# A list scheduler's priorities shifted by fixed, hashed offsets in 33 stretches of its operation list

## The chip, the cores and the metric

The kernel runs on one core of a Trainium2 chip. That core has five engines that this kernel uses: TensorE (PE in the profile, with PEld for its weight loads), VectorE (DVE), ScalarE (ACT), GpSimd (POOL), and SyncE (SP), which issues the transfers. Each engine works through its own queue of instructions in order, and engines wait for one another through semaphores. The metric is the device time of one execution in microseconds; the median over several runs is what is compared.

## The reference

Two attention layers are computed over 2048 tokens of width 1024, with 32 heads of 32, and their outputs are concatenated.

```python
# A: causal softmax attention in 4 segments of 512, plus a memory M, z carried from segment to segment
q, k, v = x @ wq, x @ wk, x @ wv                 # per head
for s in range(4):
    p = softmax(qs @ ks.T * scale + mask);  a_dot = p @ vs
    a_mem = (phi(qs) @ M) / (phi(qs) @ z + 1e-6)          # phi(t) = t + 1 if t > 0 else exp(t)
    outs.append(g * a_mem + (1 - g) * a_dot)              # g = sigmoid(beta), one a head
    M, z = M + phi(ks).T @ vs, z + phi(ks).sum()
a = concat(outs) @ wo
# B: linear attention with a learned map and two softmaxes over 32 features
pq, pk = q @ w_phi, k @ w_phi
phi_q = concat(softmax(pq), softmax(-pq));  phi_k = concat(softmax(pk), softmax(-pk))
kv, z = phi_k.T @ v, phi_k.sum()
b = ((phi_q @ kv) / (phi_q @ z + 1e-6)) @ wo
out = concat([a, b], axis=-1)
```

## The kernel before, in words

Every large product is made of float16 halves: an operand is scaled, its float16 rounding is the high half and the remainder the low half, and three products (high by high, high by low, low by high) are added in PSUM. Three of the products (q and k of B, v of B, the output of A) are also done by a Strassen scheme of seven products on half-size blocks (`strassen`, and `mult` at the end of the kernel), whose sums are made on DVE, ACT and POOL.

The work has five stages, in this order of time:

- **The opening.** Loads of x and of the first weights, their scaling into halves (`load_seg`, `load_wg`, `load_wv`, all through `halved` and `halves`), while PE runs products of the identity to keep busy (L1079).
- **Stage A.** 32 units, each one segment and one group of four heads. `produce(u)` projects q, k and v of a unit (L378) and `attend(u)` does its attention: row maxima (L796 on PE, L802 on DVE), scores (L894), exponentials (L898, L900 on ACT), masks (L907 on POOL), and the product with v (L930). In the background the weights of B are folded with the feature map (`fold`, L1035).
- **The change from A to B.** The V projection of two pairs of token blocks is taken ahead (`xpair` with the Strassen form made on POOL and ACT, L477 and L484, after a scaling at L546), while the last units of A attend.
- **The K pass of B.** Eight pairs of blocks: Strassen for k and v (L574), two softmaxes (`expo`, L1140 to L1154), and the sums over tokens (L1294). At its end the sums are turned into the operands of the next stage (L1317 and around).
- **The Q pass of B, and the output of A.** For 16 token blocks the same for q, then the transposed features times the sums (L1475), and the output projection of B (`project`, L378). Last come 8 pairs of blocks of A's output by Strassen (`mult`, L1539).

None of this order is written out engine by engine. The code calls `Graph.op` once for every operation (16,483 in all), in program order, with an engine, an expected duration, a function that emits the instructions, the buffers read and written, and a priority `prio`: a small number is to go first. In stage A the priority is 2u for `produce(u)` and 2u + 1 for `attend(u)`; in B it is 100 plus two for each pair of K, then one for each block. `Graph.op` stores `(prio, place in the list)` in `o.prio`. At the end `Graph.run` plays the whole list through in planned time: at each step it takes the engine that can start first, and of the operations that are ready there it emits the one with the smallest `o.prio`:

```python
            some = [x for x in lists[e] if start(x) <= t + 1e-9]
            if e == "PE":
                some = [x for x in some if safe(x) <= t + 1e-9] or some
            o = min(some, key=lambda x: x.prio)
```

So the priority decides only between operations that are ready at the same planned moment; data dependences, buffers and PSUM banks hold whatever the priority is. Every emission fixes a place in an engine's queue. Where the planner foresees PE idle for more than `GAP = 0.5` us, `fill` (L336) emits some products of the identity into a free PSUM bank, at most one per 0.22 us of four fifths of the gap; they compute nothing that is used. They are instructions that depend on the order.

SP's transfers stand in the same list: one queue, in planned order.

Of the kernel before, what the change touches and what calls it, by code (L numbers as in the profile page):

```python
# [41 lines left out]
WPLAN = ((None, 0, 0), (None, 2, 1), (None, 3, 5), ((1, 0, "subtract"), 0, 3), ((3, 1, "subtract"), 1, 4),  # L42
         ((3, 0, "subtract"), 3, 2), ((2, 3, "subtract"), 2, 6))
EUP = 2.0 ** 15


def view(t, off, ap):
# [13 lines left out]


class Op:
    __slots__ = ("eng", "dur", "fn", "prio", "lat", "deps", "wait", "ready", "short", "port", "banks", "place", "known", "safe", "kb")


class Graph:
# [36 lines left out]
    def op(self, eng, dur, fn, r=(), w=(), prio=0, lat=0.0, short=False, port=False, need=(), kb=256):  # L104
        o = Op()
        o.short, o.port = short, port or eng == "POOL"
        o.eng, o.dur, o.fn, o.prio, o.lat, o.kb = eng, dur, fn, (prio, len(self.ops)), lat, kb
        o.banks = []
        ends, starts = set(), set()
        for b in need:  # L110
            if b.prev[0] is not None:
                ends.update(b.prev[0].ops)
        for write, accs in ((0, r), (1, w)):
            for acc in accs:
                b, key = acc if isinstance(acc, tuple) else (acc, None)
                old, last, opened = b.prev
                if old is not None:
                    ends.update(old.ops)
                if not b.ops and last is not None:
                    starts.add(last.ops[0])  # L120
                if opened is not None:
                    starts.add(opened)
                for k in (list(b.writer) if key is None else [key, None]):
                    if k in b.writer:
                        ends.add(b.writer[k])
                if write:
                    for k in (list(b.readers) if key is None else [key, None]):
                        ends.update(b.readers.pop(k, ()))
                    if key is None:
                        b.writer.clear()  # L130
                    b.writer[key] = o
                else:
                    b.readers.setdefault(key, []).append(o)
                b.ops.append(o)
                if b.kind is not None and b not in o.banks:
                    o.banks.append(b)
                    b.left += 1
        ends.discard(o)
        o.deps = [(d, 0) for d in ends] + [(d, 1) for d in starts - ends if d is not o]
        self.ops.append(o)  # L140
        return o

# [115 lines left out]
SP, PE, ACT, DVE, POOL = "SP", "PE", "ACT", "DVE", "POOL"  # L258
# [3 lines left out]
def tile_kernel(ctx: ExitStack, tc: tile.TileContext, ax, aw, awv, awo, beta, bx, bwqk, bwv, bphi, bwo, out):  # L262
# [69 lines left out]
    for t in vfb:  # L332
# [7 lines left out]
    gate1 = const.tile([128, H], F32, name="gate1")  # L340
    gates = G.fixed(gate)
    op(SP, 0.6, lambda: nc.sync.dma_start(gate, bass.AP(tensor=beta.tensor, offset=beta.offset, ap=[[0, 128], [1, H]])),
       w=[gates], prio=0.2, lat=2.0, kb=16)
    op(ACT, 0.2, lambda: nc.scalar.activation(gate, gate, AF.Exp, bias=0.0, scale=-1.0), w=[gates], prio=0.2)
    op(DVE, 0.2, lambda: nc.vector.tensor_scalar(gate, gate, 1.0, None, op0=OP.add), w=[gates], prio=0.2)
    op(DVE, 0.3, lambda: nc.vector.reciprocal(gate, gate), w=[gates], prio=0.2)
    op(DVE, 0.2, lambda: nc.vector.tensor_scalar(gate1, gate, -1.0, 1.0, op0=OP.mult, op1=OP.add), w=[gates], prio=0.2)
# [779 lines left out]
    def expo(ps, prio, sk, up=None):  # L1127
        port = ps not in psums

        def x3():  # L1130
            return ps().rearrange("p (h d) -> p h d", d=32)

        def rep(v):
            return v[:, :, None].to_broadcast([128, 16, 32])

        mx = G.buf("b", [128, 2, 16], F32, "mx", 2)
        e = G.buf("b", [128, 16, 2, 32], F32, "e", 5)
        r = G.buf("b", [128, 16, 2], F32, "r", 5)
        for i, o in ((0, OP.max), (1, OP.min)):
            op(DVE, 0.6, lambda i=i, o=o: nc.vector.tensor_reduce(mx()[:, i, :], x3(), axis=AX.X, op=o),  # L1140
               r=[ps], w=[(mx, i)], prio=prio)
        op(DVE, 0.6, lambda: nc.vector.tensor_tensor(e()[:, :, 0, :], x3(), rep(mx()[:, 0, :]), op=OP.subtract),  # L1142
           r=[ps, (mx, 0)], w=[(e, 0)], prio=prio, port=port)
        op(DVE, 0.6, lambda: nc.vector.tensor_tensor(e()[:, :, 1, :], rep(mx()[:, 1, :]), x3(), op=OP.subtract),  # L1144
           r=[ps, (mx, 1)], w=[(e, 1)], prio=prio, port=port)
        for i in range(4):
            op(ACT, 0.41, lambda i=i: nc.scalar.activation(  # L1147
                e()[:, 4 * i:4 * i + 4], e()[:, 4 * i:4 * i + 4], AF.Exp, bias=0.0, scale=sk()[:, i:i + 1]),
               r=[e, sk], w=[(e, ("x", i))], prio=prio)
        op(DVE, 1.13, lambda: nc.vector.tensor_reduce(r(), e(), axis=AX.X, op=OP.add), r=[e], w=[r], prio=prio)  # L1150
        op(DVE, 0.27, lambda: nc.vector.reciprocal(r(), r()), r=[r], w=[r], prio=prio)
        if up is not None:
            op(POOL, 0.2, lambda: nc.gpsimd.tensor_scalar(r(), r(), up, None, op0=OP.mult), r=[r], w=[r], prio=prio)
        return e, r  # L1154

    def bc32(r):
        return r()[:, :, :, None].to_broadcast([128, 16, 2, 32])
# [84 lines left out]
    for p in range(NT // 2):  # L1242
# [9 lines left out]
        def kout(i, hb, ps, es=es, sk=sk, P=P):  # L1252
            e, r = expo(ps, P, sk, EUP)
            op(POOL, 1.95, lambda: nc.gpsimd.tensor_tensor(e(), e(), bc32(r), op=OP.mult), r=[e, r], w=[e], prio=P)
            es[i, hb] = e
# [58 lines left out]
    for q in range(4):  # L1314
        ps = bank("misc", [128, 512])
        for i in range(4):
# [3 lines left out]
        op(ACT, 0.5, lambda q=q, ps=ps: nc.scalar.activation(  # L1320
            zb()[:, 4 * q:4 * q + 4, :].rearrange("p a b -> p (a b)"), ps(), AF.Copy, scale=1.0 / EUP), r=[ps], w=[(zb, q)], prio=P)
    op(DVE, 0.1, lambda: nc.vector.tensor_scalar(osc2[:, 1, 0:1], big[:, 1:2], 2.0, None, op0=OP.mult),
# [299 lines left out]
```

## Time and profile before

| | |
|---|---|
| median of 3 runs | 1735.99 us (1734.22 to 1736.42) |
| span of the profiled execution | 1738.3 us, 2.3 us above that median |
| PE busy | 1696.5 us, 98% of the span |
| DVE busy | 1394.7 us, 80% |
| ACT busy | 1140.9 us, 66% |
| POOL busy | 961.8 us, 55% |
| mean granted TensorE clock | 0.995 of full |
| transfers | 275.71 MB, mean 159 GB/s |

The page of the profile gives, in this order, the busy time by engine, the span in 40 slices, the transfer queues, the chain of work that ended last, and the costliest groups of instructions. The same trace can be asked for the busy time of each engine in any stretch, for instructions in order of time, and for who waited for whom. A matmul is shown with the time until its result is out (380 ns for 512 columns), and the next may start before that; so a PE that is shown busy may still start fewer matmuls than it could. An idle PE is shown only where a gap is longer than that tail.

### The profile page before, as it was taken

What the parts mean: (1) busy time and instruction counts of PE and PEld (TensorE: products, weight loads), DVE (VectorE), ACT (ScalarE), POOL (GpSimd) and SP (SyncE); (2) the same over time, 40 slices, a digit from 0 to 9 for tenths busy, and PEclk for the clock granted to TensorE, in tenths of its full rate; (3) what the DMA queues carried; (4) which work ended last, traced back from release to release, by engine and by line L of the source; (5) the groups of instructions that cost most, each with busy time, mean ns of one, the idle gap of its engine ahead of it and who ended that gap; (6) DMA issues with size and microseconds to landing.
All of it is one profiled execution on the core that took longest, in us unless ns stands there. A gap on an engine that the chain in (4) does not pass through costs nothing. (4 is left out here: it accounts for less than half of the span.)

```text
span 1738.3 us, 38775 instructions
## 1 busy us (share of the span) xinstructions
PE 1696.5 (98%) x14604; PEld 1027.0 (59%) x14604; DVE 1394.7 (80%) x3197; ACT 1140.9 (66%) x2083; POOL 961.8 (55%) x1301
## 2 busy tenths in 40 slices
PE   8999999999999999999999999999999999999998
PEld 6767767667776767766754444444544444454443
DVE  6989889789878878788885999996998777696441
ACT  6987887888778776878765767654664554454331
POOL 6446354445757775867755545453588898541000
PEclk9999999999999999999999999999999999999999
DMA  6546545457544643565466443346555774576311
GB/s 203 192 133 173 154 143 177 146 163 233 153 148 136 150 130 113 161 209 149 128 202 241 141 164 128 128 164 233 217 146 146 172 193 134 128 206 171 110 65 61
DMA packets 240844, 275.71 MB, mean 159 GB/s; under 512 B 137488, under 2 KB 190480, under 8 KB 231952
## 3 DMA queue, kind: packets, MB, share of 16 engines
q1 hardware_dynamic: 240656, 273.22, 51.8%
q8 instruction: 115, 1.88, 0.5%
q14 instruction: 73, 0.60, 0.1%
HBM read 145.44 MB, written 85.00 MB: 133 GB/s over the span
## 5 line engine op out<-in xcount | busy, mean ns | idle before, releaser
L378 PE MATMUL proj<-S,S 128*128 128x512 f16 (+1 forms) x3072 | 499.8, 300 | 2.8 <-ACT S L405 0.7
L378 PEld LDWEIGHTS <-S 128*128 128x128 f16 x4608 | 330.6, 98 | 150.5 <-issue 5.5
L574 PE MATMUL proj<-S,S 128*128 128x512 f16 x1488 | 345.4, 380 | 9.2 <-ACT cs L580 4.9
L574 PEld LDWEIGHTS <-S 128*128 128x128 f16 x1968 | 187.0, 98 | 224.9 <-issue 10.4
L907 POOL TENSOR_SCALAR_AFFINE_SELECT ph<-ph 128x256 f16<-128x256 f16 (+1 forms) x448 | 193.5, 453 | 167.3 <-DVE ph L901 148.1
L901 DVE SCALAR_TENSOR_TENSOR ph<-s,ph 128x512 f16<-128x512 f32 x320 | 210.3, 684 | 66.1 <-ACT ph L900 64.0
L802 DVE CUSTOM_DVE_ANT_0 s<-s,causal 128x256 f32<-128x256 f32 (+3 forms) x512 | 242.5, 509 | 16.5 <-PE s L796 13.2
L898 ACT ACTIVATE s<-s,bd 128x512 f32<-128x512 f32 x320 | 211.8, 705 | 25.1 <-PE s L894 23.1
L900 ACT ACTIVATE ph<-s 128x512 f16<-128x512 f32 x320 | 189.3, 651 | 0.9
L378 PE MATMUL misc<-S,ot 128*128 128x512 f16 x768 | 170.7, 379 | 0.0
L1147 ACT ACTIVATE e<-e,sk 128x256 f32<-128x256 f32 x256 | 114.5, 498 | 84.8 <-DVE e L1144 81.1
L378 PEld LDWEIGHTS <-ot 128*128 128x128 f16 x768 | 73.7, 98 | 87.6
L796 PE MATMUL s<-S 96*128 96x512 f16 (+3 forms) x512 | 113.3, 299 | 3.1 <-DVE mt L802 1.5
L894 PE MATMUL s<-S 104*128 104x512 f16 (+3 forms) x512 | 113.8, 299 | 1.1 <-DVE mt L802 0.9
L1444 POOL TENSOR_TENSOR e<-e,zb 128x512 f32<-128x512 f32 x64 | 84.9, 1340 | 44.9 <-DVE r L1150 38.8
L378 PE MATMUL proj<-wv,S 128*128 128x128 f16 x1536 | 107.9, 220 | 1.0 <-DVE mt L802 0.7
L930 PEld LDWEIGHTS <-ph 128*128 128x128 f16 x2560 | 87.4, 96 | 16.6 <-issue 1.8
L930 PE MATMUL pv<-vl,ph 128*128 128x66 f16 (+1 forms) x2560 | 92.6, 184 | 1.9 <-POOL ph L907 0.8
L1150 DVE TENSOR_REDUCE r<-e 128x32 f32<-128x1024 f32 x64 | 76.7, 1203 | 15.9 <-ACT e L1147 15.8
L574 PE MATMUL s<-S,S 128*128 128x512 f16 x324 | 77.4, 379 | 0.0
L1287 POOL TENSOR_TENSOR pt<-e,pt 128x512 f16<-128x512 f32 x32 | 38.6, 1209 | 65.9 <-ACT pt L1284 63.2
L802 DVE DVE_READ_ACCUMULATOR2_ANT mt<- 128x1 f32 x512 | 71.8, 140 | 0.0
(330 smaller groups left out, 3313.1 us busy)
## 6 DMA issues: line engine op xcount, KB each, us to landing
S<-h SPq DMA_DIRECT2D x192, 128.0 KB
S<-wf_d SPq DMA_DIRECT2D x21, 1024.0 KB
st<-bwqk SPq DMA_DIRECT2D x64, 256.0 KB
wf_d<-fo SPq DMA_DIRECT2D x48, 256.0 KB
out<-os SPq DMA_DIRECT2D x39, 256.0 KB
wf_d<-oT SPq DMA_DIRECT2D x36, 256.0 KB
S<-xf_d SPq DMA_DIRECT2D x9, 1024.0 KB
S<-aw SPq DMA_DIRECT2D x16, 512.0 KB
```

The lines of the kernel that those rows point to most:

```text
L378: op(PE, dur, lambda c=c, a=a, b=b, lv=lv, rv=rv: nc.tensor.matmul(pv(), lv(), rv(), start=(c == 0 and a + b == 0), stop=(c == n - 1 and a ...
L574: op(PE, 0.215, lambda n=n, a=a, b=b, lv=lv, rv=rv: nc.tensor.matmul(ps(), lv(), rv(), start=(start and n == 0 and a + b == 0), stop=(n == ...
L796: nc.tensor.matmul(ps()[:, o:o + 128 * i + 128], st()[0:96, 0, h, 128 * i:128 * i + 128], st()[0:96, 1, h, 0:128 * i + 128], start=True, s ...
L802: dve(0.12 + 0.00113 * n, lambda h=h, i=i, o=o, n=n: nc.vector.tensor_tensor_reduce(ps()[:, o:o + n], ps()[:, o:o + n], causal[:, 512 - n: ...
L894: nc.tensor.matmul(ps()[:, o:o + n], st()[0:104, 1, h, 128 * j:128 * j + 128], st()[0:104, 0, h, 128 * j:512], start=True, stop=True)
L898: act(0.59, lambda: nc.scalar.activation(ps(), ps(), AF.Exp, bias=0.0, scale=bd()[:, 4, i2, 0:1]), r=[(bd, i2)], w=[ps])
L900: act(0.5, lambda: nc.scalar.activation(ph()[:, 0], ps(), AF.Copy, scale=2.0 ** 14), r=[ps], w=[(ph, 0)])
L901: dve(0.6, lambda: nc.vector.scalar_tensor_tensor(ph()[:, 1], ps(), 2.0 ** 14, ph()[:, 0], op0=OP.mult, op1=OP.subtract), r=[ps, (ph, 0)], ...
L907: nc.gpsimd.affine_select(pd, pd, pattern=[[0, n], [1, 128]], compare_op=OP.is_ge, fill=0.0, base=0, channel_multiplier=-1)
L930: nc.tensor.matmul(ps()[:, i, n0:n1], ph()[:, a, o:o + 128], vl()[:, j, h, n0:n1], start=(i == 0 and a == 0), stop=(j == min(i, 2)), skip_ ...
L1147: op(ACT, 0.41, lambda i=i: nc.scalar.activation(e()[:, 4 * i:4 * i + 4], e()[:, 4 * i:4 * i + 4], AF.Exp, bias=0.0, scale=sk()[:, i:i + 1 ...
L1444: op(POOL, 1.35, lambda a=a, h0=h0, e=e: nc.gpsimd.tensor_tensor(e()[:, 8 * a:8 * a + 8], e()[:, 8 * a:8 * a + 8], zv()[:, h0:h0 + 8], op= ...
```

## The change

Every operation gets an offset on its priority if it lies in one of 33 chosen stretches of 60 operations in the list. The offset is a hash of the operation's place and of the stretch's number in a table, scaled to plus or minus 0.3, 0.7, 1.5 or 3.0 (chosen by the last two bits of that number). Matmuls that follow one another with the same priority, code and bank share one place, and so one offset, so that a run of matmuls into one bank stays together. The chosen stretches are 0, 3, 4 and 5 (the opening), ten between 162 and 178 (the last units of A and the first products of B), eleven between 207 and 227 (the end of the K pass and the first blocks of Q), and eight between 251 and 260 (the last blocks of Q and the first of A's output). Durations, dependences, buffers, and the functions that emit instructions are as they were.

```diff
+STRETCH, REACH = 60, (0.3, 0.7, 1.5, 3.0)
+NUDGE = {0: 102925, 3: 583361, 4: 334074, 5: 356900, 162: 548157, 166: 12065, 167: 23722, 168: 590453, 170: 363531, 172: 857500,
...
+         254: 713827, 257: 574795, 258: 625840, 259: 632051, 260: 875719}
 class Op:
-    __slots__ = (..., "known", "safe", "kb")
+    __slots__ = (..., "known", "safe", "kb", "at", "base")
+def nudge(at):
+    seed = NUDGE.get(at // STRETCH, 0)
+    if not seed:
+        return 0.0
+    x = (at * 2654435761 & 0xFFFFFFFF) ^ (seed * 2246822519 + 374761393 & 0xFFFFFFFF)
...
+    return REACH[seed & 3] * (2 * (x / 4294967296.0) - 1)
 def op(self, eng, dur, fn, ...):
...
+        o.base, o.at = prio, len(self.ops)
+        last = self.ops[-1] if self.ops else o
+        if o.eng == "PE" and (last.eng, last.base, last.fn.__code__, last.banks) == (o.eng, prio, fn.__code__, o.banks):
+            o.at = last.at
+        o.prio = (prio + nudge(o.at), len(self.ops))
         self.ops.append(o)
```

More of the change, by code (lines that the diff above doesn't have):

```diff
@@ L63 @@
 class Op:
-    __slots__ = ("eng", "dur", "fn", "prio", "lat", "deps", "wait", "ready", "short", "port", "banks", "place", "known", "safe", "kb")
+    __slots__ = ("eng", "dur", "fn", "prio", "lat", "deps", "wait", "ready", "short", "port", "banks", "place", "known", "safe", "kb", "at", "base")
+def nudge(at):
[3 more added lines that the diff above has]
+    x = (at * 2654435761 & 0xFFFFFFFF) ^ (seed * 2246822519 + 374761393 & 0xFFFFFFFF)
+    x ^= x >> 15
+    x = x * 2246822519 & 0xFFFFFFFF
+    x ^= x >> 13
+    x = x * 3266489917 & 0xFFFFFFFF
+    x ^= x >> 16
+    return REACH[seed & 3] * (2 * (x / 4294967296.0) - 1)
 class Graph:
```

2 rows, old and new, of the table NUDGE are left out of this document.

## The prediction

> **What bounds the kernel now.** I read the busy times first, then the time in stages, then the planner's idle-time products in the same stages, then the instructions in order of time around the waits, and last the order of the two built programs. The page says PE:
>
> ```profile
> span 1738.3 us, 38775 instructions
> PE 1696.5 (98%) x14604; PEld 1027.0 (59%) x14604; DVE 1394.7 (80%) x3197; ACT 1140.9 (66%) x2083; POOL 961.8 (55%) x1301
> L336 PE MATMUL fill<-ident 128*128 128x128 f32 x148 | 23.6, 305 | 0.0
> ```
>
> PE is idle for 1738.3 − 1696.5 = 41.8 us, and 23.6 us of its busy time are fills (L336), which compute nothing. The next fence has the busy time in eight stretches, which I cut at the opening and the changes of stage, and the same for fills alone. The columns are length, then busy us and count for PE, PEld, DVE, ACT and POOL, the granted clock, the transfers' share and GB/s; the fills' rows have PE and PEld only.
>
> ```profile
> 0.00:40.00 40.00, 35.15 (x251) 26.90 (x252) 26.39 (x69) 28.39 (x40) 25.16 (x36) 0.96 0.58 191
> 40.00:870.00 830.00, 818.98 (x8947) 583.55 (x8945) 713.26 (x2070) 656.09 (x1191) 501.38 (x798) 1.00 0.54 158
> 870.00:930.00 60.00, 54.57 (x425) 33.15 (x424) 43.73 (x103) 40.17 (x71) 40.70 (x56) 0.94 0.62 199
> 930.00:1220.00 290.00, 281.87 (x1824) 138.04 (x1823) 251.77 (x412) 175.21 (x353) 133.66 (x125) 1.00 0.48 173
> 1220.00:1305.00 85.00, 80.35 (x628) 45.15 (x627) 80.86 (x137) 53.72 (x114) 58.35 (x62) 1.00 0.56 170
> 1305.00:1520.00 215.00, 214.31 (x1391) 101.15 (x1389) 164.07 (x241) 106.17 (x188) 175.03 (x197) 1.00 0.61 155
> 1520.00:1580.00 60.00, 58.16 (x403) 29.40 (x401) 47.76 (x67) 27.67 (x47) 27.51 (x31) 1.00 0.66 177
> 1580.00:1738.27 158.27, 153.07 (x749) 69.61 (x747) 66.82 (x99) 53.46 (x82) 0.00 (x0) 1.00 0.29 103
> ...
> 0.00:40.00 40.00, 4.41 (x22) 3.74 (x22) 0.96 0.58 191
> 870.00:930.00 60.00, 7.18 (x40) 6.44 (x40) 0.94 0.62 199
> 930.00:1220.00 290.00, 1.05 (x8) 1.05 (x8) 1.00 0.48 173
> 1220.00:1305.00 85.00, 7.24 (x50) 6.20 (x50) 1.00 0.56 170
> 1520.00:1580.00 60.00, 3.71 (x28) 3.52 (x28) 1.00 0.66 177
> ```
>
> The reader should see that PE's loss, idle time plus fills, is dense in short places. From A to B it is 5.43 + 7.18 = 12.6 us in 60; from K to Q 4.65 + 7.24 = 11.9 in 85; from Q to A's output 1.84 + 3.71 = 5.6 in 60; in the opening 4.85 + 4.41 = 9.3 in 40. Stage A and the K pass lose 11.0 and 8.1 us of idle time spread over 1120 us, and 1305 to 1520 only 0.7. DVE is busy 80.86 of 85 us from K to Q, so there it, and not PE, sets the pace.
>
> What ends the waits in these places (start, duration, engine, line; idle time before it and its releaser in brackets):
>
> ```profile
> 896.57 2.03 PE L336 MATMUL fill<-ident 128*128 128x128 f32 x16
> 899.59 1.12 PE L574 MATMUL proj<-S,S 128*128 128x512 f16 x4 [1.00 <-ACT S L484]
> 902.03 0.59 PE L822 MATMUL misc<-identr,mh 128*8 128x128 f16 x4 [1.32 <-DVE mh L817]
> 902.55 2.08 PE L336 MATMUL fill<-ident 128*128 128x128 f32 x8
> 897.89 1.13 ACT L546 ACTIVATE wv<-wv,pst 128x1024 f32<-128x1024 f32 x1
> 898.92 1.65 ACT L484 ACTIVATE S<-wv 128x512 f16<-128x512 f32 x3
> ...
> 1266.03 0.38 SPq L561 DMA_DIRECT2D S<-xf_d  x1
> 1273.49 2.76 PE L574 MATMUL proj<-S,S 128*128 128x512 f16 x12 [1.15 <-DMA S<-xf_d]
> 1283.85 2.05 PE L336 MATMUL fill<-ident 128*128 128x128 f32 x16
> 1550.12 1.83 PE L336 MATMUL fill<-ident 128*128 128x128 f32 x14
> 1568.97 2.75 PE L1539 MATMUL proj<-S,S 128*128 128x512 f16 x12 [1.46 <-ACT S L1556]
> ```
>
> From A to B, PE sits through 8 fills (16 passes, since a float32 product takes two) and 1.00 us more until ACT has scaled the second x block (L546) and rounded its first forms (L484). From K to Q it waits for a transfer that SP issues at 1266.03. At the end of Q it fills between the blocks' sums and output products.
>
> **What the change moves.** All 16,483 planned operations stay, so no work is removed but fills. Their order was compared in the built programs: on PE, 8140 of 9740 operations have another place (by at most 228); on DVE 2452 of 2675, on ACT 1745 of 1988, on POOL 1037 of 1286, on SP 600 of 793 (by at most 19). The first PE move is at its 67th operation, and everything after that follows, chosen stretch or not. The fills, counted as instructions by place:
>
> ```
>                     opening  stage A  A to B  K pass  K to Q  Q to out   all
> fills before           11       0       20      4      25       14       74
> fills after            11       2        4      4      15        0       36
> ```
>
> A fill stands only where the planner found no ready PE work for over 0.5 us, so the new order has ready work in about half of those places. That is no time; I price it by the rows.
>
> *Opening: 0.* The fills stay 11. On PE, the first v product moves behind the second half of the q product. On POOL, five small operations (three of L351, one L764, one L727) move ahead of the second weight group's halves.
>
> ```profile
> 34.63 1.16 POOL L402 TENSOR_TENSOR S<-S,S 128x512 f16<-128x512 f32 x1 [1.38 <-ACT S L401]
> 38.84 2.27 POOL L402 TENSOR_TENSOR S<-S,S 128x512 f16<-128x512 f32 x2
> 41.22 1.27 POOL L764 TENSOR_TENSOR pk<-pk,z 128x512 f32<-128x512 f32 x1
> 43.16 2.55 POOL L351 TENSOR_TENSOR bdm<-hd,gate 128x128 f32<-128x128 f32 x7
> 45.68 0.57 POOL L727 TENSOR_SCALAR sc<-gate,bv 128x4 f32<-128x4 f32 x2
> 40.42 0.81 PE L378 MATMUL proj<-S,S 128*128 128x512 f16 x3
> 47.94 4.48 PE L378 MATMUL proj<-S,S 128*128 128x512 f16 x20
> ```
>
> They cost 3 × 0.36 + 1.27 + 0.29 = 2.6 us. The first half group was ready at 34.63 + 1.16 = 35.8 and is wanted at 40.42; the second was ready at 38.84 + 2.27 = 41.1 and is wanted by 47.94. Both slacks, 4.6 and 6.8, cover 2.6. If L764, now ahead, also waits for its exponential, the cover of the first is gone and PE waits up to 2 us. I take 0, with ends −1 (the q half done earlier) and +2.
>
> *A to B: −5.7.* L546 stands 32 to 34 places earlier on ACT, its scale matmul (L521) 75 places earlier on PE, and the first products of V (L574) 88 to 106 places earlier; the key update of the unit before (L869) stands 70 later, ready work for the gap. On POOL the last fold's forms (L477, L485) move up to 28 places back and the second V pair's up to 28 ahead, for the same PE products; SP's transfers here move by at most 8 places. So the wait at 896 to 900 loses its cause. 16 fills fewer × 7.18 / 20 = 5.7 us. At best half of the 5.43 us idle there (2.7) and the lost clock go too (60 × 0.06 = 3.6): −12. At worst the waits stay without fills: 0.
>
> *K to Q: −2.9.* The sums (L1294, L1317) are mixed with Strassen products; 10 fills fewer × 7.24 / 25 = 2.9. The transfer at 1266.03 keeps its place in SP's queue: here only two stores move by more than 2 places. So the 1.15 us stay, and the 8 fills before the first output products (L378) are still there. Ends: 0, and −5 with half of the idle time.
>
> *Q to A's output: −3.7.* All 14 fills go; the output products (L378) now stand between the sums (L1475) and the first products of A's output. 3.71 us; ends 0 and −4.6 (with half of 1.84).
>
> *Stage A and the K pass: +0.6, and a new draw.* Two new fills × 23.6 / 74 = 0.6. Besides, 11.0 + 8.1 = 19.1 us of small waits fall anew, since these orders change too. I see no direction in it; between a quarter less and a quarter more, ±5. The longest of them also slowed the clock:
>
> ```profile
> 336.40 1.08 PE L864 MATMUL misc<-ident,pk 128*128 128x128 f32 x4 [2.57 <-DVE mt L802]
> 340.00:342.00 2.00, 2.00 (x8) 0.76 (x6) 1.38 (x4) 0.00 (x0) 0.00 (x0) 0.50 0.81 151
> 304.22:347.68 43.46, 40.47 (x430) 27.56 (x428) 34.72 (x93) 36.09 (x67) 20.19 (x40) 0.92 0.46 146
> ```
>
> After 2.57 us of waiting PE ran at half clock; the slice lost 0.08 × 43.46 = 3.5 us of clock.
>
> *Sum.* 0 − 5.7 − 2.9 − 3.7 + 0.6 = −11.7, the fills' own time. PE does not get all of it: where a fill goes, a short wait under 0.5 us can stand, which the planner does not count. In the trace idle time outside the opening and the tail (41.8 − 4.85 − 5.2 = 31.8) is larger than the fills outside the opening (23.6 − 4.41 = 19.2), so more waits are unforeseen than foreseen. I take off a third: −8. The end does not move: after 1580 PE is full (its 5.2 us idle is the last store) and in both programs the same products remain. 1738.3 − 8 = 1730.3 for the profiled execution; it stood 2.3 above the median, so 1728.0.
>
> **Rivals.**
> *The waits go with their fills, and more.* All better ends: −1 − 12 − 5 − 4.6 − 5 = −27.6, around 1708; half of that beyond the forecast is 1718. For it: the bracketed waits lie beside the fills that go. Against: DVE at 80.86 of 85 us.
>
> *Nothing that counts.* The gain in three places, −8, is given back by the new draw, +5, and the opening, +2: 1735. For it: 84% of PE's operations move, so waits that the old order happened to hide can open anywhere in 1120 us, and from K to Q DVE is full whatever PE's order is.
>
> *Slower: the waits stay, the fills go, and the clock falls.* Place: 870 to 930 and 1220 to 1305. Without fills PE idles where it was kept busy, and each half-clock stretch costs what the slice above lost, 3.5 us. With two or three more of them, +7 to +10: 1743 to 1746. It decides from the point at which PE's idle time in these two places exceeds its present 10.1 us by the 8.6 us that the fills gave up. Against it: the L546 move takes the cause of the longest wait away. [...]
>
> **How the numbers follow.** Forecast (1721 to 1732): 0.55. More (below 1721): 0.17. Nothing that counts (1732 to 1740): 0.13, of which 0.02 and 0.01 lie just outside the bound that follows. Slower (above 1740): 0.15. What a measurement of this kernel can tell from no change is about 0.2%, 3.5 us: 1732.5 to 1739.5. Faster 0.74, same 0.10, slower 0.16. The range 1715 to 1740 leaves out the outer part of the second case (0.05) and the last one (0.15).
>
> **What would show it.** Fills of about 72 passes and 11 to 12 us. From A to B no wait for L484 above 1 us and a clock near 1.00. K to Q still with a wait for xf_d and DVE full. No fills and no wait for L1556 at the end of Q. Wrong would be: PE's idle time in the three places above 15 us, a new half-clock stretch, or a wait over 2 us for POOL's weights near 40 us.

## The result and the profile after

The changed kernel takes 1726.93 us (median of 4 runs, 1723.14 to 1728.99) against 1735.58 us for the kernel before (median of 4, 1734.22 to 1736.42). The ratio is 0.9947, with a 95% interval of 0.9933 to 0.9962: 6.6 to 11.6 us less. The forecast was 1728.0.

The head of the changed kernel's page (lines of this kernel stand 24 further down: L360 is the fill that was L336):

```profile
span 1721.4 us, 38599 instructions
PE 1682.5 (98%) x14528; PEld 1014.9 (59%) x14528; DVE 1397.0 (81%) x3197; ACT 1145.5 (67%) x2083; POOL 966.6 (56%) x1301
```

The eight stretches of the prediction, cut where PE had done the same matmul work, with the columns as there:

```profile
0.00:40.50 40.50, 33.64 (x259) 25.91 (x260) 26.67 (x73) 29.60 (x42) 25.52 (x39) 1.00 0.64 202
40.50:867.40 826.90, 817.62 (x8877) 580.06 (x8876) 713.42 (x2069) 659.31 (x1191) 500.41 (x794) 1.00 0.53 159
867.40:916.70 49.30, 47.19 (x422) 29.17 (x421) 40.40 (x98) 39.35 (x70) 35.73 (x51) 1.00 0.62 205
916.70:1210.80 294.10, 284.47 (x1849) 139.85 (x1848) 253.22 (x412) 173.55 (x348) 138.74 (x133) 0.99 0.49 174
1210.80:1295.30 84.50, 77.54 (x619) 42.89 (x617) 83.51 (x145) 54.24 (x119) 56.28 (x61) 1.00 0.57 184
1295.30:1509.70 214.40, 214.40 (x1393) 101.22 (x1392) 172.84 (x248) 108.72 (x192) 181.19 (x200) 1.00 0.63 167
1509.70:1564.30 54.60, 54.60 (x374) 26.18 (x374) 38.56 (x56) 27.48 (x44) 28.70 (x30) 1.00 0.53 148
1564.30:1721.39 157.09, 153.10 (x750) 69.65 (x747) 68.34 (x101) 53.25 (x81) 0.00 (x0) 1.00 0.28 101
```

And the fills alone, in the stretches that have any (PE and PEld only):

```profile
0.00:40.50 40.50, 3.32 (x22) 2.84 (x22) 1.00 0.64 202
40.50:867.40 826.90, 0.69 (x4) 0.52 (x4) 1.00 0.53 159
867.40:916.70 49.30, 1.05 (x8) 0.97 (x8) 1.00 0.62 205
916.70:1210.80 294.10, 1.22 (x8) 1.21 (x8) 0.99 0.49 174
1210.80:1295.30 84.50, 4.25 (x30) 3.73 (x30) 1.00 0.57 184
```

The stretch from A to B is 49.3 us long instead of 60, and the one at the end of Q 54.6 instead of 60, with PE busy in all of it. The K pass is longer, 294.1 instead of 290. From K to Q DVE is busy 83.51 of 84.5 us, against 80.86 of 85.

The two profiled executions differ by 16.9 us, twice what the runs differ by. The changed one is the fastest of its four runs; the one of before, at 1738.3, was slower than every one of that kernel's four runs. So single stretches of two profiles are read here only together with the runs.

For that I use one more quantity. A matmul's usual step is the distance between starts that the kernel before shows when nothing is in the way (216 ns for 512 columns). **Loss** is the start time of a matmul minus the steps of all matmuls before it; fills count as no work. So it holds waits, fills and time at a lower clock together. All kernels below do 1641.1 us of steps, so losses can be compared at the same work. The table has the loss that each stretch adds; "open" is the first 250 us of steps (the opening and the first units of A), then the marks are 800, 900, 1150, 1300 and 1450 us of steps. Each row is one execution; the last column is the ratio of times to the kernel before, from several runs.

```
                 fills  open    A   A-B     K   K-Q    Q   end    all    ratio (95%)
before              74  19.9  20.6  16.2  12.9  14.7  2.3   4.8   91.3
after               36  23.7  14.0   6.0  16.9  13.3  1.4   0.4   75.7   0.9947 (0.9933-0.9962)
opening alone       91  25.7  16.0  16.7   8.1  15.3  2.5   4.5   88.7   1.0004 (0.9995-1.0013)
A to B alone        60  19.4  16.1  12.8  14.5  14.5  2.3   4.7   84.2   0.9981 (0.9973-0.9990)
K to Q alone        56  19.4  16.9  14.0  11.1  13.3  1.4   2.8   78.9   0.9969 (0.9957-0.9981)
end of Q alone      60  20.4  18.4  14.7  12.3  14.6  1.5   0.4   82.3   0.9966 (0.9953-0.9979)
K to Q + end        46  20.2  17.8  16.0  11.9  13.3  1.5   0.4   81.0   0.9949 (0.9935-0.9962)
all but opening     31  20.4  18.4  13.2  12.5  13.4  1.7   0.4   79.9   0.9938 (0.9925-0.9950)
```

In the changed kernel's row the loss falls most in stage A, from A to B and at the end, and it rises before 250 us of steps and in the K pass. Its 75.7 against 91.3 is more than the runs differ by, since these are the two profiled executions above.

### The profile page after: what moved, and what is told of

Its sections match the earlier page's. It is cut to its first block, busy times and chain, and to the rows that moved or that the text cites. A ratio compares the mean times of both kernels' runs of the same rounds, so it can differ in the third digit from the quotient of the medians.

```text
span 1721.4 us, 38599 instructions
## 1 busy us (share of the span) xinstructions
PE 1682.5 (98%) x14528; PEld 1014.9 (59%) x14528; DVE 1397.0 (81%) x3197; ACT 1145.5 (67%) x2083; POOL 966.6 (56%) x1301
## 4 chain that ended last, share of the span: by engine, by line
PE 68%; DVE 18%; ACT 5%; POOL 4%; issue 3%; DMA 3%; SPq 0%; DVEq 0%; POOLq 0%; ACTq 0%
PE proj L402 20%; PE proj L598 11%; PE misc L402 10%; PE proj L1563 5%; PE s L918 3%; PE s L820 3%; DVE s L826 3%; PE pv L954 3%; PE s L1563 2%; DVE ph L925 2%; DVE mx L1164 1%; PE pv L1499 1%; PE s L598 1%; DVE r L1174 1%; PE misc L1563 1%
## 5 line engine op out<-in xcount | busy, mean ns | idle before, releaser
L402 PE MATMUL proj<-S,S 128*128 128x128 f16 (+1 forms) x3072 | 500.0, 299 | 1.8 <-ACT S L429 0.7
L826 DVE CUSTOM_DVE_ANT_0 s<-s,causal 128x512 f32<-128x512 f32 (+3 forms) x512 | 242.7, 510 | 22.6 <-PE s L820 19.3
L402 PE MATMUL proj<-wv,S 128*128 128x128 f16 x1536 | 100.4, 219 | 0.3 <-DVE wgs L415 0.3
L954 PEld LDWEIGHTS <-ph 128*128 128x128 f16 x2560 | 87.8, 96 | 19.4 <-POOL ph L931 2.7
L772 ACT ACTIVATE h<-proj,bd 128x512 f16<-128x512 f32 x64 | 46.6, 734 | 44.4 <-PE proj L402 44.2
```

Of the source, the lines that this page charges most:

```text
L402: op(PE, dur, lambda c=c, a=a, b=b, lv=lv, rv=rv: nc.tensor.matmul(pv(), lv(), rv(), start=(c == 0 and a + b == 0), stop=(c == n - 1 and a ...
L826: dve(0.12 + 0.00113 * n, lambda h=h, i=i, o=o, n=n: nc.vector.tensor_tensor_reduce(ps()[:, o:o + n], ps()[:, o:o + n], causal[:, 512 - n: ...
L954: nc.tensor.matmul(ps()[:, i, n0:n1], ph()[:, a, o:o + 128], vl()[:, j, h, n0:n1], start=(i == 0 and a == 0), stop=(j == min(i, 2)), skip_ ...
```

## The experiments

**Each place alone.** Four kernels, each with the table cut to one group of stretches; nothing else differs.

```diff
-NUDGE = {... all 33 ...}
+NUDGE = {... the 10 from 162 to 178 ...}      # A to B;  likewise 0 to 5, 207 to 227, 251 to 260
```

A to B alone:

> Offsets only in the ten stretches from A to B. Theory 1 (each place's waits are its own): stage A as before, the loss at the change from A to B falls from about 16 us to 2 to 6, the K pass is redrawn by up to 4 us either way, the rest as before: 5 to 9 us under the kernel before. Theory 2 (the gain is a new draw of small waits everywhere, begun by the opening): within 3 us of the kernel before, since the opening and stage A keep their order.

It measured 1732.14 us against 1735.40 (11 and 24 runs), ratio 0.9981 (0.9973 to 0.9990): 3.3 us less, between theory 1's 5 and theory 2's 3. By the interval (1.7 to 4.7 us) it is a gain, but it decides neither theory. In this kernel, and the others whose table is cut, lines stand 21 further down than before. The stretch from A to B in its profile:

```profile
865.10:919.90 54.80, 49.24 (x391) 28.02 (x389) 42.02 (x101) 37.89 (x67) 35.61 (x49) 0.94 0.58 181
```

PE in order of time in it, the rows with the longest waits and with fills:

```profile
882.95 0.38 PE L915 MATMUL s<-S 104*128 104x384 f16 x2 [2.59 <-DVE ph L922]
886.41 2.29 PE L595 MATMUL proj<-S,S 128*128 128x512 f16 x5 [1.01 <-DVE ph L922]
893.75 0.83 PE L357 MATMUL fill<-ident 128*128 128x128 f32 x6
903.27 0.59 PE L915 MATMUL s<-S 104*128 104x512 f16 x3 [1.29 <-ACT S L845]
```

Of 40 passes of fills 6 are left, and the wait for the x forms (L484) is gone. A wait of 2.59 us for DVE (L901 of the kernel before) stands in their place, with no fill ahead of it, so it seems that the planner had not foreseen it. PE is idle for 54.80 − 49.24 = 5.56 us, as much as the 5.43 of before.

The end of Q alone:

> Offsets only in the eight stretches at the end of Q. Theory 1: everything up to about 1500 us as before, no fills and no wait for L1556 between 1520 and 1580: 3 to 5 us under the kernel before. Theory 2: within 2 us of it.

1729.57 us, ratio 0.9966 (0.9953 to 0.9979): 5.8 us less, 0.8 above the range of theory 1. This is the clearest place. Its profile in the stretch that lost 5.6 us before:

```profile
1516.20:1571.00 54.80, 54.80 (x354) 25.88 (x353) 40.57 (x57) 26.63 (x43) 28.12 (x31) 1.00 0.61 147
```

PE has no idle time in it, and no fill. The loss at the end falls from 4.8 to 0.4 in every kernel with these offsets.

K to Q alone:

> Offsets only in the eleven stretches from K to Q. Theory 1: 1 to 3 us under the kernel before, the wait for xf_d still there. Theory 2: within 2 us of it.

1730.73 us, ratio 0.9969 (0.9957 to 0.9981): 4.7 us between the medians, more than either theory said. The place itself gave 14.7 − 13.3 = 1.4 us of loss. DVE is fuller than before:

```profile
1211.60:1296.10 84.50, 77.53 (x618) 42.88 (x617) 83.53 (x146) 53.76 (x119) 56.30 (x61) 1.00 0.57 184
```

PE's fills from K to Q take less time, but PE is idle there for 84.50 − 77.53 = 6.97 us, against 4.65 before: waits that the planner had not covered took part of what the fills gave up. Another 2.0 (4.8 to 2.8) came at the end of Q, 200 us later, where this kernel has no offsets: the order there follows from the one before it.

The opening alone:

> Offsets only in the four stretches of the opening. Theory 1: the opening itself 2 to 4 us worse (the wait for the first halves at 37 us), the wait of 2.57 us near 336 us and its half clock gone, the change from A to B redrawn with 31 fills against 20: 0 to 6 us over the kernel before. Theory 2: this holds most of the gain, 4 to 8 us under the kernel before.

1736.13 us, ratio 1.0004 (0.9995 to 1.0013): no difference. Theory 2 falls. Its loss by 250 us of steps is 25.7, against 19.4 to 20.4 in the kernels without the opening's offsets; the rest of A (16.0, against 16.1 to 20.6) and the K pass (8.1, against 11.1 to 14.5) give it back. One place where the opening loses is seen in the changed kernel:

```profile
33.77 3.57 PE L402 MATMUL proj<-wv,S 128*128 128x128 f16 x61
37.18 0.59 PE L402 MATMUL proj<-S,S 128*128 128x512 f16 x2
39.72 0.59 PE L820 MATMUL s<-S 96*128 96x512 f16 x3 [1.95 <-DMA S<-h]
```

PE waits 1.95 us for the transfer of the first unit's k and q (S from h). The v products that lay over this transfer are done by then; the kernel before had them at the end:

```profile
36.12 4.46 PE L378 MATMUL proj<-wv,S 128*128 128x128 f16 x77
```

This wait is not the whole loss. By 30 us of steps the changed kernel has lost only 0.5 us more than the kernel before, and the opening alone 2.8 us more; about 3 us come later, between 125 and 250 us of steps, where PE is idle more often: 3.97 us between 150 and 250 us, against 0.98. The kernel before and, below it, the changed kernel:

```profile
150.00:250.00 100.00, 99.02 (x1061) 71.23 (x1061) 88.78 (x262) 80.83 (x146) 43.06 (x76) 1.00 0.57 168
150.00:250.00 100.00, 96.03 (x1025) 68.14 (x1024) 88.47 (x258) 85.22 (x155) 50.16 (x84) 1.00 0.52 154
```

In exchange the wait of 2.57 us near 336 us is gone: between 300 and 350 us of steps both kernels with the opening's offsets lose under 0.3 us, and the kernel before 6.1.

**Do the places add up?** Two more cuts of the table.

```diff
-NUDGE = {... all 33 ...}
+NUDGE = {... the 29 from 162 on ...}          # and: the 19 from 207 on
```

> All offsets but those of the opening. Theory 1 (places add up): the gains of the three places alone, 3.3 + 4.7 + 5.9 us, less some 2 us that K to Q and the end of Q both took from 1500 to 1560, so 11 to 13 us under the kernel before and 2 to 4 us under the changed one. Theory 2 (the opening's new order of stage A is what lets the change from A to B gain): 3 to 6 us over the changed kernel, since the wait of 2.6 us for DVE at L901 that the A to B offsets showed alone stays.

1724.87 us, ratio 0.9938 (0.9925 to 0.9950): 10.9 us under the kernel before, where theory 1 had 11 to 13, and 2.1 under the changed kernel, where it had 2 to 4 and theory 2 a loss. The opening's offsets are not needed for the gain. From A to B its loss is 13.2, as with A to B alone, against 6.0 in the changed kernel; but the changed kernel gives 4.4 of that back in the K pass and 3.3 before 250. (The totals of these two rows can't be set against each other: here the slowest of five runs was profiled, and the fastest of four of the changed kernel.)

> Offsets only from K to Q and at the end of Q. Theory 1: 4.7 + 5.9 less 2, so 8 to 10 us under the kernel before, as much as the whole change: then opening and A to B bring nothing together. Theory 2: 3 to 5 us over the changed kernel, because A to B with the opening's order is worth that much.

1727.93 us, ratio 0.9949 (0.9935 to 0.9962): the same as the whole change. So the opening and A to B together bring nothing that these runs can tell, although A to B is where the two first profiles differ most. The K pass of the changed kernel has longer waits than before, and loses 4.0 us more (PE in order of time):

```profile
1003.62 0.49 PE L1318 MATMUL kv<-ot,pt 128*128 128x64 f16 x11 [3.56 <-DVE ot L1204]
1078.87 0.83 PE L360 MATMUL fill<-ident 128*128 128x128 f32 x6
1082.13 1.19 PE L598 MATMUL proj<-S,S 128*128 128x512 f16 x4 [2.43 <-ACT S L429]
```

Around the first of them, the stretch of 10 us (the granted clock is the third number from the end):

```profile
1000.00:1010.00 10.00, 6.44 (x34) 2.72 (x32) 7.42 (x11) 2.94 (x5) 2.76 (x3) 0.83 0.75 254
```

The longest, 3.56 us for the low halves of v, is followed by a lower clock, 0.83 over these 10 us; the longest wait for the same tile in the kernel before's K pass is 1.6 us. It belongs to the order, not to one execution: the two kernels below that have this order of work and fewer fills wait 3.55 and 3.56 us there. That it follows from the gain from A to B is not shown.

**Is the move of L546 the cause from A to B?** There are two V pairs, and each has two scalings (L546) on ACT. The kernel before:

```profile
815.90 1.15 ACT L546 ACTIVATE wv<-wv,pst 128x1024 f32<-128x1024 f32 x1
818.21 1.14 ACT L546 ACTIVATE wv<-wv,pst 128x1024 f32<-128x1024 f32 x1
896.31 1.15 ACT L546 ACTIVATE wv<-wv,pst 128x1024 f32<-128x1024 f32 x1
897.89 1.13 ACT L546 ACTIVATE wv<-wv,pst 128x1024 f32<-128x1024 f32 x1
```

The changed kernel:

```profile
787.39 2.19 ACT L570 ACTIVATE wv<-wv,pst 128x1024 f32<-128x1024 f32 x2 [0.23 <-DVE pst L549]
888.00 2.27 ACT L570 ACTIVATE wv<-wv,pst 128x1024 f32<-128x1024 f32 x2
```

Counted in the order of ACT's starts in the two traces, the first pair's stand 32 and 34 places earlier, and the second pair's 4 and 5. The wait at 896 to 900 ends with the second pair's. So the move of 32 to 34 places that the prediction counted on is that of the other pair. The next kernel makes that move alone: in the kernel before, only the priority of the first V pair's preparation is changed.

```diff
-XL = (5, -0.2)
+XL = (7, -0.2)
```

> The kernel before, with only the first V pair's preparation (L546 and what leads to it) put forward by two units of priority. If that move alone lifts the change from A to B, the wait for L484 at 899 goes and the kernel is 4 to 8 us under the kernel before. If it takes the whole set of moves there, the waits go elsewhere: its order has 26 fills in that place against 20, so 0 to 4 us over the kernel before.

1743.24 us against 1736.11, ratio 1.0041 (1.0028 to 1.0054): 7.1 us slower, more than either bound. On ACT the first pair now stands within two places of where the changed kernel has it, and the second pair within one place of where it was:

```profile
786.74 1.30 ACT L546 ACTIVATE wv<-wv,pst 128x1024 f32<-128x1024 f32 x1
898.98 2.19 ACT L546 ACTIVATE wv<-wv,pst 128x1024 f32<-128x1024 f32 x2
```

PE no longer waits for L484 near 899, but it still waits for the second pair, now for the input of its scale product (L521), and then for the last units of A (PE in order of time):

```profile
891.74 2.39 PE L336 MATMUL fill<-ident 128*128 128x128 f32 x20
895.73 0.35 PE L521 MATMUL misc<-wm,xt 128*128 128x2 f32 x2 [1.60 <-DVE xt L519]
905.14 0.37 PE L930 MATMUL pv<-vl,ph 128*128 128x66 f16 x8 [1.27 <-DVE ph L901]
909.45 3.34 PE L336 MATMUL fill<-ident 128*128 128x128 f32 x14
```

The first pair's move by itself is no gain. That its earlier work keeps DVE, ACT and POOL from the units of A is likely, but not shown. The second pair put forward alone was not tried.

**What are the fills worth?** Both kernels without any fill; nothing else in the order changes.

```diff
-    G.filler = lambda ps: nc.tensor.matmul(ps, ident, ident, start=True, stop=True)
+    G.filler = None
```

> The kernel before without its 74 fills, the order otherwise the same. Theory 1 (fills stand in waits that are there anyway): within 2 us of the kernel before; PE idle grows by about 20 us and PE busy falls by 23. Theory 3 (fills hold the clock): 4 to 12 us slower, with two or more new stretches at half clock from 895 to 925 and 1243 to 1290.

1744.81 us against 1735.77, ratio 1.0044 (1.0030 to 1.0057): slower by 9.0 us between the medians, so theory 3 holds for this order. The wait that the fills had covered comes out whole, and the clock falls (PE in order of time):

```profile
900.69 1.89 PE L574 MATMUL proj<-S,S 128*128 128x512 f16 x4 [2.88 <-ACT S L484]
```

The stretch around it:

```profile
898.00:930.00 32.00, 24.11 (x159) 12.67 (x160) 18.37 (x36) 19.68 (x35) 27.14 (x34) 0.74 0.62 193
```

The granted clock over these 32 us is 0.74, against 0.89 from 898 to 930 in the kernel before. Over the whole span it is 0.988 to 0.992 in the five runs, against 0.995 to 0.998 in the nine of the kernel before beside them. The order of all other instructions is the same in both traces, so nothing but the fills differs.

> The changed kernel without its 36 fills. Theory 1: within 2 us of the changed kernel. Theory 3: 2 to 6 us slower, half as much as for the kernel before, with new half-clock stretches in the opening and near 1060 to 1290.

1723.78 us, ratio 0.9930 (0.9918 to 0.9943). This order does not need its fills: without them it is no slower, and the medians differ by 3.2 us the other way, with overlapping intervals. The mean clock is lower all the same, 0.993 to 0.995 in its five runs against 0.996 to 0.998 in the changed kernel's four. Two more kernels asked whether the opening's fills are worth keeping while the later ones cost queue time:

```diff
     def fill(self, s, t, banks, work):
+        if s > 60:
+            return
```

> All offsets but the opening's, and fills in the first 60 planned us only (11 of 31 stay). If late fills cost more queue time than their clock is worth, as the changed kernel without fills suggests, 1 to 3 us under the same order with all fills, so 3 to 5 us under the changed kernel. If the late fills hold the clock, 2 to 5 us over that order, with more half clock near 885 and 1270.

1725.25 us, ratio 0.9936 (0.9924 to 0.9948), against 0.9938 with all fills.

> The changed kernel with fills in the first 60 planned us only (11 of 36 stay). The opening's fills were worth some 2 to 4 us in the first 250 us of PE work in both pairs with and without fills, so 1 to 4 us under the changed kernel without any fills, 3 to 6 under the changed kernel. If the gain without fills was chance, within 1.5 us of the changed kernel.

1726.29 us, ratio 0.9949 (0.9936 to 0.9963), against 0.9947 with all and 0.9930 with none. Both say that the late fills of these orders change nothing that can be measured. The expectation that they cost queue time falls, and the 0.9930 is not told apart from chance.

**Would any offsets have done?** The same stretches and reaches with other numbers in the table.

```diff
-NUDGE = {0: 102925, 3: 583361, ..., 260: 875719}
+NUDGE = {0: 653157, 3: 267853, ..., 260: 13751}
```

> The same 33 stretches and reaches with other numbers in the table, so other offsets; this order has 129 fills against 74 before and 36 after. If the count of fills tells the time as it did for the changed kernel (38 fewer, 8.6 us less), 55 more give 8 to 17 us over the kernel before, with PE's losses from 1500 to 1580 (25 fills) and at about 1360 to 1420 (26 fills, where the kernel before has none). If any offsets would have done, within 4 us of the changed kernel.

1772.35 us against 1736.11, ratio 1.0206 (1.0192 to 1.0220): 36 us slower, beyond what the fills said. The group of its fills:

```profile
L360 PE MATMUL fill<-ident 128*128 128x128 f32 x258 | 37.1, 285 | 0.0
```

And PE in order of time in the Q pass, where the kernel before has almost no waits:

```profile
1380.45 2.39 PE L360 MATMUL fill<-ident 128*128 128x128 f32 x20
1384.89 0.86 PE L1499 MATMUL pv<-pt,st 128*64 128x128 f16 x24 [1.88 <-DMA pt<-kls]
1424.13 0.81 PE L1499 MATMUL pv<-pt,st 128*64 128x128 f16 x22 [2.70 <-DMA pt<-kls]
```

So not any offsets do; one other table can't say how rare a good one is. The orders tried here span 47 us, most of it on the slow side. The fills tell the direction: of the ten orders measured, the four with 74 fills or more (74, 82, 91, 129) are the four slowest, and the three fastest have 31, 36 and 46. They don't tell the size: 17 more for the opening alone cost nothing, 8 more with the pair put forward 7 us.

**A version that beats both?** All but the opening, 0.9938 or 0.9936, has the lowest medians of the orders with fills, 1724.87 and 1725.25, but its interval overlaps the changed kernel's. It is not shown to be faster.

## Why the prediction came out right, and where its steps failed

The total was right: −8 us forecast, −8.6 measured. Of its parts the end of Q was right in cause; the others were wrong in size, path or cause. That the total came within 1 us all the same is in good part luck. It is not the clock that made the gain: the four runs have 0.996 to 0.998, and the 24 runs of the kernel before in the first comparison 0.996 in the mean, so the clock gives about 1 us, an estimate from these means.

**The fills as a sign.** "The new order has ready work in about half of those places" held: 72 passes and 10.53 us of fills (11 to 12 forecast), and the waits that they stood in went at the end of Q and from A to B. The discount by a third was needed: −11.7 lies just outside the interval of 6.6 to 11.6 us. Its reason was seen in one place only. From K to Q the fills fell by 3.0 us (7.24 to 4.25) and PE's idle time rose by 2.3 (4.65 to 6.96); in the other two places idle time fell with the fills (5.43 to 2.11, 1.84 to 0). So that reason accounts for little of the discount; losses that rose elsewhere, 3.8 us before 250 us of steps and 4.0 in the K pass, weigh as much or more.

**Opening, 0 (−1 to +2).** Right for the whole kernel, +0.7 us alone with an interval of −0.9 to +2.3, but by luck: in both kernels of the table with these offsets they cost 3 to 6 us of loss before 250 us of steps, more than the step's range, and where they stand alone this came back later in A and in the K pass, of which the step does not speak. The feared wait for POOL's weights did not come; a wait of 1.95 us for the transfer of k and q did, which the step had not named. It had counted the moved v products as free, and they were the cover of that transfer.

**A to B, −5.7.** The largest term, and the step that failed. Alone it measured −3.3 us (−1.7 to −4.7), and beside the other two places −1.9 (0.9938 against 0.9949, intervals overlapping). "So the wait at 896 to 900 loses its cause" rests on a move of 32 to 34 places that is the first V pair's, while the wait is for the second pair, which moved by 4 and 5. The wait did go, but the first pair's move alone made the kernel 7.1 us slower. What makes the changed kernel's 6.0 us of loss here, against 12.8 with the same offsets alone, is the order of stage A that the opening leaves behind; which part of it was not separated. Two more executions of that order, with fewer fills, have a loss of about 6 and 7 us here, so it is no chance of one execution.

**K to Q, −2.9.** Measured −4.7 between the medians, but by another path. The place gave 1.4, half of the term, as a full DVE let one think; 2.0 came at the end of Q and 0.9 in between. The wait for the transfer of x was forecast to stay and did not: in the changed kernel PE waits there for ACT and DVE instead (1.33 us for ACT at 1272).

**Q to A's output, −3.7 (0 to −4.6).** Right in cause and a little small: −5.8 (−3.6 to −8.2), no fill, no wait for L1556, PE full. The loss fell by 4.4.

**Stage A and the K pass, +0.6 and ±5.** The K pass drew 4 us more of loss in the changed kernel (16.9 against 12.9), near the edge of that range, about as much as A to B gained in this table beyond its term. The prediction had no direction for it, and none is seen: the opening alone drew 4.8 less there. One of the prediction's signs of being wrong, a new stretch at a lower clock, stands here (0.83 over 1000 to 1010, where the kernel before has 1.00); in exchange, the stretches of 0.86 near 336 us and 0.94 from A to B are at 1.00 in the changed kernel.

**The rivals.** "Slower: the waits stay, the fills go, and the clock falls" is seen here in one kernel: the kernel before without fills is 9.0 us slower with its clock at 0.988 to 0.992. It did not decide here: PE's idle time from A to B and from K to Q is 2.11 + 6.96 = 9.1 us, and it would have had to exceed the 10.1 of before by 8.6. Taking the fills out lowered the mean clock of the old order from 0.995 to 0.998 down to 0.988 to 0.992, and that of the new order from 0.996 to 0.998 down to 0.993 to 0.995; in the new order the time does not rise measurably (1723.78 us without fills, 1726.93 with them).

## What to carry to other kernels

Where PE is 98% busy and a planner sets the order, look for idle time and filler in the short stretches between stages; a new order there was worth 0.3% in each of two places alone, and the two together were worth as much as the whole change. Price such a change as a whole: what one stretch gained, others lost. When a line of the code runs for several blocks, make sure that the instruction that moved is the one that the wait was for; here it was not, and that move made alone cost 7 us. Two profiles that differ by twice what the runs differ by cannot be read stretch by stretch; several executions of the same order can.

## What the runs showed of the hardware

The same wait does not cost the same each time. Five executions share the order of stage A up to the wait near 336 us, and each waits 2.56 or 2.57 us for the same row maximum. The granted clock over the 25 us around it was 0.86, 0.93, 0.86, 1.00 and 0.93 (the kernel before, A to B alone, the end of Q alone, K to Q alone, K to Q and the end). The kernel before:

```profile
325.00:350.00 25.00, 22.01 (x215) 14.88 (x211) 19.59 (x62) 17.63 (x32) 9.09 (x15) 0.86 0.58 190
```

A to B alone, and its wait:

```profile
325.00:350.00 25.00, 22.04 (x208) 15.26 (x206) 20.15 (x65) 19.01 (x34) 9.47 (x16) 0.93 0.57 182
335.65 1.09 PE L885 MATMUL misc<-ident,pk 128*128 128x128 f32 x4 [2.56 <-DVE mt L823]
```

K to Q alone, and its wait:

```profile
325.00:350.00 25.00, 22.01 (x212) 15.12 (x210) 21.05 (x70) 20.48 (x37) 10.83 (x20) 1.00 0.58 187
335.51 0.63 PE L885 MATMUL misc<-ident,pk 128*128 128x128 f32 x4 [2.57 <-DVE mt L823]
```

0.14 of 25 us is 3.5 us of clock. The loss follows it: between 308 and 330 us of steps it is 6.3, 4.8, 6.2, 3.4 and 4.8 us, in the same order. That is 2.9 of the 4.5 us by which the loss of stage A differs among these executions (16.1 to 20.6). After the same wait the clock over the 25 us is lower by 0.14 in two of the five executions, by 0.07 in two, and not at all in one; what decides which was not shown. So part of the spread between these executions is the clock around one and the same wait.
